# A written-out instruction order replaced in a fused attention and feed-forward kernel on Trainium2, with a new rule for its filler products

## The chip, the cores and the metric

The kernel runs on one core of one Trainium2 chip. The metric is the device time of one execution in microseconds (us); the median of three runs of the kernel before is 267.36 us (266.87 to 269.35). [...]

## The reference, cut to what matters

Eight batches, eight heads, 576 rows of 64 elements. The attention goes by 32 landmarks (the means of 18 rows each), a pseudo-inverse by six Newton steps, and a two-layer network follows on all 4608 rows of 512 elements.

```python
A  = softmax(scale * q @ k_lm.T)          # 576 x 32
Bm = softmax(scale * q_lm @ k_lm.T)       # 32 x 32
C  = softmax(scale * q_lm @ k.T)          # 32 x 576
Z  = Bm.T / (norm1(Bm) * norminf(Bm) + 1e-6)
for _ in range(6):
    Z = 2 * Z - Z @ Bm @ Z
x = A @ Z @ C @ v                         # per head, then heads side by side
h = x @ w_in                              # 512 -> 2048
out = relu(h) ** 2 @ w_out                # 2048 -> 512
```

## The kernel before, in words

The program is a list of named operations. `Plan.op` records each with its engines and what it reads and writes; `Plan.schedule` walks the long string `ORDER`, gives each name a start by a table of costs, and sorts by that start; then each engine's instructions are emitted in that order. A word `R2.7/D` puts the operation on VectorE, `/A` on ScalarE, `/P` on GpSimd; `@2,0` names the banks of the accumulator memory (eight in all). So the string decides three things: the order on every engine, which engine does an operation that has a choice, and which bank is used.

Per batch b the operations are, by name: `ldq`, `ldk`, `ldv`, `lx` (loads, all issued by GpSimd, 16-bit copies of 32-bit inputs), `lm`, `lmc`, `lme`, `lmt` (landmark sums, their copies and transposition), `T` (VectorE transposition of q and k), `B..` (softmax of Bm and its norms), `bd`, `N`, `U` (one Newton step: block-diagonal copy, product, update), `SS` or `SC`, `SA` (scores), `C..` and `A..` (their softmaxes), `CV`, `Zm`, `ZC`, `W`, `We` (the chain C v, Z C v, and its product with w_in, copied to the tile WP). Then the network: `Fb.f` is a group of four products of AT and WP (line 1023), `R` the relu that takes it out of the accumulator (ScalarE line 1037, VectorE line 1039), `Q` the square (line 1046 on VectorE or GpSimd, line 1044 on ScalarE). `Ot.g` is a quarter of the second layer for one tile of 128 rows: four products of 512 columns (line 1063), `Oe` its copy out, `St` its store. Groups `O` of an earlier batch are placed between the groups `F` and the attention of a later one, so that TensorE has work while the other engines do softmaxes.

Constants are made at the start: `c0` and `c1` (memsets of ones, lines 320 and 321), `c2` (GpSimd's affine select that makes the identity, line 322), `c3` (its 16-bit copy, line 325), `c5` (two selects that make a mask, lines 330 and 332). The first landmark product `lm0.1` (line 480) needs that identity, the load `ldq0.1` and the load `ldk0.1`.

Between the kernel's own products stand products of a constant tile of ones (line 1137) that nobody reads, so that TensorE is not idle at the start. `Plan.fillers` chooses them: it takes every gap of the planned TensorE times up to the first group `O0.0`, and fills it with as many as fit.

Of the kernel before, what the change touches and what calls it, by code (L numbers as in the profile page):

```python
# [7 lines left out]
P = 128  # L8
# [45 lines left out]
class Plan:  # L54
# [100 lines left out]

    def fillers(self, until, width, emit):

        busy = sorted((o.start, o.start + o.engs["PE"] + 0.04) for o in self.ops if o.eng == "PE")
        found, at = [], 1.5
        for a, b in busy:  # L160
            if a > until:
                break
            n = int((a - 0.05 - at) / (width if at > 6 else 2 * width))
            if n > 0:
                for j in range(8):
                    if all(h[1] >= a or h[2] <= at - 0.02 for h in self.history if h[0] == j):
                        found.append((at, j, n))
                        break
            at = max(at, b)
        for at, j, n in found:  # L170
            o = Op()
            o.name, o.eng, o.start, o.mode = f"fill{at:.0f}", "PE", at, "full"
# [1003 lines left out]
lmt1.0 bk1/P win20 ldk2.1 B1@4 Asb0.1a ldv1.00 U0.1 Bmx1 Asu0.1b N0.2@0 Arc0.0b U0.2 Bsb1 Aex0.1a
Bex1 CR0@7 CRe0/A Asu0.1a N0.3@6 U0.3 N0.4@7 Bsu1 Arc0.1a CT0.0 U0.4 Brc1 Aex0.0a Asu0.0a Bmb1
Bml1 N0.5@7 U0.5 Arc0.1b Blo1 CV0@0,4 Btr1 Aml0.0b Arc0.0a c14/A CVe0.0/A Bcs1@3 Zd0@6 Zm0
CVe0.1/A ZC0@0 BBT1@2 ZCe0 Aml0.0a Bnm1 T1.01 Bad1 Brn1 Aml0.1b Ap0.0@3 Ab0.0/A SA1.1@6 Aml0.1a
Zi1 Yi1 T1.11 W0.0@0 We0.00 We0.01 N1.0@5 W0.1@2 We0.1 U1.0 T1.10 N1.1@4 U1.1 F0.2@0 R0.2 Amx1.1  # L1180
N1.2@5 U1.2 ldv1.10 Q0.2/P wout0 F0.0@2 R0.0 wout1 Asb1.1 Aex1.1 SC1.0@4,0 Cmx1.1 Ap0.1@2 Ab0.1/A
Cex1.1 N1.3@7 U1.3 Cmx1.0 Cex1.0 SA1.0@6 Amx1.0 N1.4@7 U1.4 Asb1.0 F0.4@2 F0.16@0 R0.4 R0.16
N1.5@7 U1.5 Crc1 W0.3@4 We0.3 Asu1.1 Cmk1 Arc1.1 Aml1.1 F0.18@6 F0.6@0 CR1@2 CRe1 F0.22@4 Q0.16/A
Q0.0/P R0.6 Q0.4/P R0.18/D CT1.0 CT1.1 R0.22 Q0.22/A F0.12@2 R0.12 Aex1.0 W0.2@0 We0.2/D Ap1.1@6
Ab1.1 lm2.0@4 lmc2.00 lmc2.01 lme2.0 CV1@2,0 CVe1.0/A CVe1.1/A F0.20@6 Zd1@2 T2.11 Zm1 F0.26@4
wout2 Q0.6/P R0.20 Q0.20/A F0.10@0 R0.10 ZC1@2 T2.10 ZCe1.0/D lmt2.0 F0.8@6 wout3 Q0.18/P R0.8
lx3.0 Q0.12/P R0.26 Q0.10/A ldv3.11 lx3.1 ldv2.00 ldq3.1 Q0.8/P O1.0@3 F0.14@0 ZCe1.1/D W1.1@6
B2@4 Asu1.0 Arc1.0 Aml1.0 Bmx2 O0.0@2 O0.1 We1.1 Q0.26/A R0.14 Bsb2 Bex2 Bsu2 Brc2 Bml2 Btf2 T2.01
Q0.14 Bcs2 Bct2 Bnm2 Bad2 Brn2 Zi2 W1.2@4 W1.3@6 W1.0@0 We1.2 We1.01 We1.3 We1.00 Btr2/A bt2/D
O1.1 O0.2 Ap1.0@4 F0.28@6 R0.28/D Q0.28/P O1.2 Ab1.0/A F1.0@0 R1.0 F0.24@4 R0.24 T2.00 BBT2@6 Yi2  # L1190
Q0.24 O1.3 Oe1.0 F1.2@0 R1.2/D F0.30@4 St1 R0.30 Q1.0/A F1.6@6 F1.8@0 bd2.0 N2.0@4 U2.0 bd2.1 R1.6
O2.0@5 O0.3 N2.1@4 F1.14@6 Q1.2/A R1.8 U2.1 Q1.8 ldk3.0 bd2.2/D O2.1 N2.2@4 Oe0.0 F1.12@2 F1.4@0
Q0.30/A R1.4 R1.14/D U2.2 bd2.3/D N2.3@4 U2.3 Q1.6 R1.12 O2.2 ldv3.10 bd2.4 ldk3.1 ldv2.11 ldq3.0
lm3.0@4 lme3.0/D lmt3.0 ldv2.10 lx4.0 N2.4@0 U2.4 bd2.5/D Q1.4/A Q1.12/A F1.18@6 R1.18 Q1.18/A
O2.3 F1.10@6 R1.10 Oe2.0 N2.5@4 B3@2 Q1.14 F1.24@0 F1.20@6 Bmx3 Bsb3 U2.5 Bex3 Bsu3 Brc3 Bml3 Btf3
Bcs3 R1.24 Q1.10/A ldv3.00 lx4.1 Zm2.0 Btr3 O3.0@3 O3.1 R1.20 Q1.20/A Q1.24/A SS2.0@0,4,6 T3.10
O5.0@2 O5.1 At2.0 Zm2.3 Amx2.0 Asb2.0 Aex2.0 SS2.1@6 Cmx2.1 Cmx2.0 Cex2.1 At2.1 Cex2.0 Bct3 Bnm3
T3.01 T3.00 Bad3 Crc2.1 Zm2.1 Amx2.1 Cnr2.1 CT2.1 Asb2.1 T3.11 O5.2 O3.2 O3.3 F1.26@6 R1.26 Oe3.0
F1.30@0 F1.22@4 Asu2.0 R1.30/D Crc2.0 F1.16@6 R1.16 Q1.16/A R1.22 O5.3 O4.0@7 O4.1 Aex2.1 Asu2.1
St2 St0 F1.28@4 O4.2 O4.3 Arc2.0 Zm2.2 Arc2.1 Aml2.0 Q1.22/A Oe5.0 R1.28 Q1.30/A Q1.26/A Oe4.0  # L1200
SS3.0@4,0,2 O7.0@6 O7.1 At3.0 Aml2.1 SS3.1@2 Cnr2.0/A CT2.0 At3.1 O6.0@7 O6.1 bt3 BBT3@2 O7.2
Cmx3.1 Ab2.1 Brn3 Yi3 Q1.28/A Cex3.1 CV2@2,0 Cmx3.0 Cex3.0 Amx3.0 Zi3 O7.3 CVe2.0 CVe2.1/A ZC2@0
ZCe2.0/D ZCe2.1 ldk4.0 ldq4.0 bd3.0 ldq5.1 N3.0@1 U3.0 Ab2.0 lm4.0@2 lx5.0 Oe7.0 St4 St5 St3
W2.0@4 We2.0 W2.1@0 We2.1 bd3.1/D N3.1@3 U3.1 bd3.2/D lme4.0/D O6.2 F2.2@4 R2.2 F2.1@2 R2.1 lmt4.0
Crc3.0 Amx3.1 Asb3.1 F2.0@0 R2.0 Q2.0 Q2.1/A O6.3 N3.2@6 U3.2 W2.2@2 W2.3@4 We2.3 We2.2 B4@0
# [24 lines left out]
Q4.2/A Q4.3/A Q4.4/A Cmx5.0 Cex5.0 Cmx5.1 Cex5.1 O17.0@6 O17.1 B6@4 Bmx6 O17.2 Bsb6 Bex6 O16.3  # L1230
Oe16.0 St16 F4.6@2 R4.6 Crc5.0 Cnr5.0 Bsu6 Brc6 N5.5@0 U5.5 Crc5.1 Bml6 F4.5@4 O17.3 F4.8@2 Amx5.1
# [70 lines left out]
```

## Time and profile before

| | us |
|---|---|
| median of three runs | 267.36 |
| lowest and highest | 266.87, 269.35 |
| the profiled execution's own time | 268.07 |
| its span in the trace | 266.3 |
| TensorE busy | 254.8 |
| VectorE busy | 210.7 |
| ScalarE busy | 185.9 |
| GpSimd busy | 75.1 |

In the profile's rows PE is TensorE, PEld its weight loads, DVE is VectorE, ACT is ScalarE, POOL is GpSimd and SP is SyncE, which issues the stores. A busy TensorE is one that has a product in its pipeline, not one at its peak. A row of the view by stretches gives, for each engine, busy time and the number of instructions, then the granted TensorE clock as a share, the share of the sixteen DMA engines, and GB/s. The chain of waits is the work that ended last, followed back from the last instruction.

### The profile page before, as it was taken

Reading aid. Unit: us, or ns where it says so; the run is one execution under the profiler, and the core shown is the slowest. Engines: PE = TensorE matmul, PEld = TensorE weight load, DVE = VectorE, ACT = ScalarE, POOL = GpSimd, SP = SyncE. Lnnn points to the kernel's source line nnn. Section 1 sums busy time; section 2 is a strip of 40 time slices with the busy share of each in tenths; the row PEclk is TensorE's granted clock in tenths of the full one; section 3 lists DMA queues with packets and bytes.
Section 4 is the critical chain, followed back from the end, with each engine's and each line's share of the span. In section 5 each row is a group of like instructions: output and inputs, shape, how many; then the busy total and the mean of one; then the engine's idle time right before and its main releaser. Section 6 shows DMA issues by size and latency. Waiting matters only on the chain.

```text
span 266.3 us, 7555 instructions
## 1 busy us (share of the span) xinstructions
PE 254.8 (96%) x3090; PEld 140.4 (53%) x3090; DVE 210.7 (79%) x539; ACT 185.9 (70%) x339; POOL 75.1 (28%) x121
## 2 busy tenths in 40 slices
PE   7699899999999999999999999999999999999993
PEld 2265566466454566455444556456454555456552
DVE  3399999856899889897998889888899895787311
ACT  1055599978687799899597759899586847667120
POOL 8445389346400362026423220210032102000000
PEclk9799999999999999999999999999999999999999
DMA  5999999997998699919996993213250330017016
GB/s 89 195 196 208 203 201 190 205 182 116 157 234 160 120 165 210 182 41 186 225 224 104 193 178 98 47 15 79 51 114 2 83 81 0 2 34 164 2 47 151
DMA packets 25123, 34.18 MB, mean 128 GB/s; under 512 B 2432, under 2 KB 14464, under 8 KB 25088
## 3 DMA queue, kind: packets, MB, share of 16 engines
q0 software_dynamic: 19168, 24.25, 55.7%
q1 hardware_dynamic: 5840, 9.38, 13.8%
q8 instruction: 24, 0.39, 0.6%
q10 hardware_dynamic: 80, 0.07, 0.1%
q14 instruction: 11, 0.09, 0.1%
HBM read 48.50 MB, written 9.44 MB: 218 GB/s over the span
## 4 chain that ended last, share of the span: by engine, by line
PE 73%; DVE 13%; ACT 6%; issue 3%; DMA 3%; POOL 0%; DVEq 0%; POOLq 0%; ACTq 0%
PE ps L1063 40%; PE ps L1023 20%; ACT RS L1037 3%; DMA X<-in_k_dram 3%; PE ps L859 2%; PE ps L702 2%; DVE TT L442 2%; PE ps L788 2%; ACT G L1044 2%; PE ps L1137 1%; DVE sm L740 1%; DVE WP L388 1%; DVE ST L680 1%; PE ps L666 1%; DVE An L938 1%
## 5 line engine op out<-in xcount | busy, mean ns | idle before, releaser
L1063 PE MATMUL ps<-w_out,G 128*128 128x512 bf16 (+1 forms) x592 | 138.5, 374 | 0.1
L1063 PEld LDWEIGHTS <-G 128*128 128x128 bf16 x592 | 54.1, 98 | 53.3 <-issue 5.4
L1023 PE MATMUL ps<-AT,WP 128*128 128x288 bf16 (+2 forms) x512 | 75.0, 286 | 0.9 <-DVE AT L996 0.3
L1037 ACT ACTIVATE RS<-ps 128x576 bf16<-128x576 f32 (+2 forms) x97 | 60.9, 652 | 19.3 <-PE ps L1023 12.0
L1023 PEld LDWEIGHTS <-WP 128*128 128x128 bf16 x512 | 47.9, 98 | 23.8 <-issue 4.3
L1044 ACT ACTIVATE G<-RS 128x576 bf16<-128x576 bf16 (+2 forms) x78 | 52.3, 687 | 0.7
L603 POOL TENSOR_TENSOR BD<-ST,blkb 128x256 bf16<-128x256 bf16 x21 | 14.9, 710 | 85.6 <-DVE ST L680 44.1
L384 ACT COPY OS<-ps 128x512 f32<-128x512 f32 (+2 forms) x29 | 16.2, 567 | 16.7 <-PE ps L1063 16.5
L442 DVE STREAM_TRANSPOSE TT<-X 128x576 uint32<-128x576 uint32 x32 | 23.8, 758 | 5.1 <-DMA X<-in_k_dram 2.8
L1039 DVE TENSOR_SCALAR RS<-ps 128x576 bf16<-128x576 f32 (+2 forms) x31 | 23.1, 754 | 5.4 <-PE ps L1023 5.1
L384 ACT CAST WP<-ps 128x1024 bf16<-128x1024 f32 (+1 forms) x25 | 22.8, 949 | 3.3 <-PE ps L859 3.2
L743 ACT ACTIVATE C<-ps,sm 128x576 bf16<-128x576 f32 x16 | 14.2, 905 | 12.8 <-DVE sm L740 10.8
L1046 DVE TENSOR_TENSOR G<-RS 128x576 bf16<-128x576 bf16 (+2 forms) x42 | 18.8, 452 | 3.6 <-ACT RS L1037 3.4
L680 DVE SCALAR_TENSOR_TENSOR ST<-ST,ps 128x128 bf16<-128x128 bf16 (+1 forms) x48 | 12.7, 264 | 8.2 <-PE ps L666 8.0
L1137 PE MATMUL ps<-onesb 128*128 128x512 bf16 (+1 forms) x40 | 14.1, 470 | 1.8 <-DVE onesb L320 1.5
L413 POOL DMA_DIRECT2D V<-in_v_dram x24 | 13.0, 543 | 7.5 <-DMA X<-in_q_dram 3.5
L388 DVE COPY OS<-ps 128x512 f32<-128x512 f32 (+1 forms) x9 | 5.8, 640 | 10.8 <-PE ps L1063 9.4
L740 DVE TENSOR_REDUCE sm<-ps 128x1 f32<-128x576 f32 x16 | 11.7, 747 | 1.6 <-PE ps L702 1.6
L976 DVE STREAM_TRANSPOSE SA<-ps 128x320 f32<-128x320 f32 (+1 forms) x24 | 10.1, 459 | 3.5 <-PE ps L697 2.4
L603 POOL TENSOR_TENSOR BD<-Bt,blkb 128x256 bf16<-128x256 bf16 x4 | 3.0, 744 | 30.9 <-DVE sm L597 15.0
L1046 POOL TENSOR_TENSOR G<-RS 128x512 bf16<-128x512 bf16 (+1 forms) x8 | 8.8, 1101 | 9.3 <-DVE RS L1039 5.9
L388 DVE CAST WP<-ps 128x1024 bf16<-128x1024 f32 x9 | 10.8, 1205 | 0.8 <-PE ps L859 0.8
(139 smaller groups left out, 303.9 us busy)
## 6 DMA issues: line engine op xcount, KB each, us to landing
out_dram<-OS SPq DMA_DIRECT2D x70, 128.0 KB, 2.4
X<-in_q_dram POOLq DMA_DIRECT2D x16, 288.0 KB, 9.2
X<-in_k_dram POOLq DMA_DIRECT2D x16, 288.0 KB, 9.3
XS<-in_q_dram POOLq DMA_DIRECT2D x5, 576.0 KB, 11.0
XS<-in_k_dram POOLq DMA_DIRECT2D x5, 576.0 KB, 10.2
V<-in_v_dram POOLq DMA_DIRECT2D x8, 288.0 KB, 10.0
w_in<-in_moe_w_in_dram POOLq DMA_DIRECT2D x8, 256.0 KB, 10.6
w_out<-in_moe_w_out_dram POOLq DMA_DIRECT2D x4, 512.0 KB, 10.2
```

The source lines that it names most:

```text
L384: nc.scalar.copy(o, i)
L388: eng(e).tensor_copy(o, i)
L442: op(f"T{b}.{t}{r}", {"DVE": v_(576)}, lambda e, r=r: nc.vector.transpose(tt[:, t, r].rearrange("p s m e -> p (s m e)").bitcast(U32), x[:, ...
L603: bdiag = lambda e, o, i: eng(e).tensor_tensor(o.rearrange("p r (c m) -> p r c m", c=4), i.unsqueeze(2).to_broadcast([P, 2, 4, M]), blkb[: ...
L680: nc.vector.scalar_tensor_tensor(out=o, in0=i0, scalar=2.0, in1=bank(pN)[:, 0:2 * w].rearrange("p (r w) -> p r w", r=2), op0=ALU.mult, op1 ...
L1023: nc.tensor.matmul(ps[:, ph.at + i, 0:w], lhsT=wp[:, r, 128 * ff:128 * ff + 128], rhs=at[:, r, t0:t0 + w], start=(r == 0), stop=(r == 1))
L1037: nc.scalar.activation(rs, pair(ph, w), AF.Relu)
L1039: nc.vector.tensor_scalar(out=rs, in0=pair(ph, w), scalar1=0.0, scalar2=None, op0=ALU.max)
L1044: nc.scalar.activation(g, rs, AF.Square)
L1046: eng(e).tensor_tensor(g, rs, rs, ALU.mult)
L1063: nc.tensor.matmul(bank(po)[:, 0:c1 - c0], lhsT=G[:, f, lo:lo + P], rhs=w_out[:, f, c0:c1], start=(f == 0), stop=(f == NF - 1))
L1137: nc.tensor.matmul(ps[:, j, 0:w], lhsT=onesb[:, 0:P], rhs=onesb[:, 0:w], start=True, stop=True)
```

## The change

Three things are changed. The string `ORDER` is replaced as a whole: 1421 names that stand in both, in another order, and some on another engine or bank. In it the identity's select `c2` stands behind the second load. The rule of `fillers` is replaced: it gives each TensorE operation a weight (`USE`), looks at windows of 3.41 us of the plan, and adds products to the widest gap of the emptiest window until each window's weighted share is 0.42 or no gap is left.

```diff
+    USE = {"N": 0.06, "M": 0.06, "B": 0.06, "Bce": 0.28, "Bcs": 0.3, "BBT": 0.08, "SC": 0.2, "CR": 0.06, "lm": 0.48,
+           "SA": 0.78, "CV": 0.63, "Zd": 0.6, "ZC": 0.2, "Ap": 0.54, "W": 0.9}
     def fillers(self, until, width, emit):
-        busy = sorted((o.start, o.start + o.engs["PE"] + 0.04) for o in self.ops if o.eng == "PE")
-        found, at = [], 1.5
-        for a, b in busy:
-            if a > until:
-                break
-            n = int((a - 0.05 - at) / (width if at > 6 else 2 * width))
...
+        times = [6.5 + 0.25 * i for i in range(int(4 * (until - 10)))]
+        for _ in range(80):
+            t = min(times, key=share)
+            near = [g for g in gaps if t <= g[0] < t + 3.41 and g[3] - g[0] - g[1] * g[4] > -0.05]
+            if share(t) >= 0.42 or not near:
                 break
+            g = max(near, key=lambda g: g[3] - g[0] - g[1] * g[4])
+            g[1] += 1
...
-c0 ldq0.1 c1 c2 ldk0.1 c3 lm0.1@2 lmc0.10 c12 T0.01 c17 Bce0@5 ldq0.0 ldk0.0 ldq1.0 ldk1.0 c5
+c0 ldq0.1 c13 c17 ldk0.1 ldq0.0 ldk0.0 ldq1.0 c1 c5 Bce0@0 c2 c3 lm0.1@2 c12 c6 c15 ldk1.0 ldk1.1
```

Behind the new rule line numbers are 19 higher, 18 at the end of the file: line 397 before is line 416 after.

On GpSimd, at the start of the program, before:

```order
6 L397 DMA X_62<-in_q_dram 128x1152
7 L322 ISA
8 L322 AFFINE_SELECT identf<-onesf 128x128
9 L397 DMA X_62<-in_k_dram 128x1152
10 L397 DMA X_62<-in_q_dram 128x1152
11 L397 DMA X_62<-in_k_dram 128x1152
12 L397 DMA X_63<-in_q_dram 128x1152
```

and after:

```order
6 L416 DMA X_62<-in_q_dram 128x1152
7 L416 DMA X_62<-in_k_dram 128x1152
8 L416 DMA X_62<-in_q_dram 128x1152
9 L416 DMA X_62<-in_k_dram 128x1152
10 L416 DMA X_63<-in_q_dram 128x1152
11 L349 ISA
12 L349 AFFINE_SELECT msel<-onesf 128x4
13 L351 AFFINE_SELECT msel<-msel 128x4
14 L341 AFFINE_SELECT identf<-onesf 128x128
```

The string names the select behind the second load, but its planned start puts it behind five loads and the mask's two selects.

On TensorE, right behind the first landmark product, before (`Bce` is line 569; four products of ones):

```order
98 L480 MATMUL ps<-X_62,ident 64x128
99 L569 MATMUL ps<-tiny,onesf 128x64
100 L1137 LDWEIGHTS onesb
101 L1137 MATMUL ps<-onesb 128x512
102 L1137 LDWEIGHTS onesb
103 L1137 MATMUL ps<-onesb 128x512
104 L1137 LDWEIGHTS onesb
105 L1137 MATMUL ps<-onesb 128x512
106 L1137 LDWEIGHTS onesb
107 L1137 MATMUL ps<-onesb 128x512
108 L702 LDWEIGHTS LT_75
```

and after, from the third product of ones on:

```order
102 L1156 LDWEIGHTS onesb
103 L1156 MATMUL ps<-onesb 128x512
104 L1156 LDWEIGHTS onesb
105 L1156 MATMUL ps<-onesb 128x512
106 L1156 LDWEIGHTS onesb
107 L1156 MATMUL ps<-onesb 128x512
108 L1156 LDWEIGHTS onesb
109 L1156 MATMUL ps<-onesb 128x512
110 L1156 LDWEIGHTS onesb
111 L1156 MATMUL ps<-onesb 128x256
112 L721 LDWEIGHTS LT_75
```

There are now six products of 512 columns and one of 256 in this place, and `Bce` stands behind the program's very first product of ones. Ahead of the landmark product are eleven of 512 and one of 256, where thirteen stood. In all there are 33 of 512 and 9 of 256, where 33 and 7 stood.

On VectorE, from the first Newton state of batch 2 (`ST_0_97<-ps`) on, before:

```order
131 L627 TENSOR_TENSOR ST_0_97<-ps,sm_118 128x2x32
132 L1046 TENSOR_TENSOR G<-RS_125 128x2x320
133 L1039 TENSOR_SCALAR RS_127<-ps 128x512
134 L680 TENSOR_SCALAR ST_1_98<-ST_0_97,ps 128x128
135 L680 TENSOR_SCALAR ST_0_97<-ST_1_98,ps 128x128
136 L1046 TENSOR_TENSOR G<-RS_127 128x2x256
137 L603 TENSOR_TENSOR BD_101<-ST_0_97,blkb 128x256
138 L1039 TENSOR_SCALAR RS_127<-ps 128x512
139 L680 TENSOR_SCALAR ST_1_98<-ST_0_97,ps 128x128
```

and after:

```order
134 L646 TENSOR_TENSOR ST_0_97<-ps,sm_118 128x2x32
135 L1058 TENSOR_SCALAR RS_127<-ps 128x512
136 L1065 TENSOR_TENSOR G<-RS_126 128x2x256
137 L1058 TENSOR_SCALAR RS_125<-ps 128x640
138 L1065 TENSOR_TENSOR G<-RS_125 128x2x320
139 L699 TENSOR_SCALAR ST_1_98<-ST_0_97,ps 128x128
140 L622 TENSOR_TENSOR BD_102<-ST_1_98,blkb 128x256
141 L699 TENSOR_SCALAR ST_0_97<-ST_1_98,ps 128x128
142 L622 TENSOR_TENSOR BD_101<-ST_0_97,blkb 128x256
```

VectorE takes one relu and one square more ahead of the first Newton update (line 680, then 699), and one block-diagonal copy that GpSimd made before.

More of the change, by code (lines that the diff above doesn't have):

```diff
@@ L1176 @@
[L1176 to L1193, printed above, removed]
@@ L1267 @@
+St34 St35 St31 Oe32.0 St32 O35.5 O35.6 O35.7 Oe35.2 Oe35.3 St35.2 St35.1
 """
```

199 lines of the change are left out of this document (114 added, 85 removed).

## The prediction

> **What bounds the kernel now.** I read the page's head first, then busy time by stretches, then the chain of waits and the timeline of the first 17 us. The head (busy time of TensorE; the chain's shares by engine):
>
> ```profile
> span 266.3 us, 7555 instructions
> PE 254.8 (96%) x3090; PEld 140.4 (53%) x3090; DVE 210.7 (79%) x539; ACT 185.9 (70%) x339; POOL 75.1 (28%) x121
> ...
> PE 73%; DVE 13%; ACT 6%; issue 3%; DMA 3%; POOL 0%; DVEq 0%; POOLq 0%; ACTq 0%
> ```
>
> TensorE is busy nearly throughout and carries 73% of the chain; VectorE carries 13%. An average says nothing about place, so busy time by stretches comes next (the second number is the stretch, then each engine's busy time and count):
>
> ```profile
> 45.00:60.00 15.00, 14.80 (x137) 8.59 (x136) 11.26 (x29) 13.11 (x24) 6.83 (x10) 1.00 1.14 194
> 60.00:70.00 10.00, 10.00 (x132) 5.75 (x131) 6.68 (x24) 8.76 (x16) 6.38 (x12) 1.00 0.85 131
> 70.00:92.00 22.00, 21.96 (x306) 10.45 (x305) 20.35 (x50) 15.81 (x30) 3.08 (x5) 1.00 0.94 175
> 92.00:109.20 17.20, 16.92 (x231) 10.66 (x231) 16.07 (x45) 16.27 (x29) 6.24 (x11) 1.00 1.07 182
> 109.20:132.00 22.80, 22.75 (x242) 12.31 (x241) 18.94 (x51) 18.69 (x33) 8.71 (x14) 1.00 0.79 150
> 144.50:174.00 29.50, 28.89 (x403) 15.55 (x402) 25.72 (x68) 23.79 (x43) 6.36 (x10) 1.00 0.70 128
> ```
>
> From 45 us on TensorE hardly idles. The stretch from 92 to 109 us differs: VectorE and ScalarE are both busy for 16 of 17.2 us, so there they set the pace. To learn how much a better order could win at all, I count TensorE's own work behind 50 us from pieces of the chain (start, duration, what):
>
> ```profile
> 50.85 1.83 PE ps L1063 x8
> ...
> 89.77 0.77 PE ps L458 x24
> ...
> 109.18 0.49 PE ps L1023 x4
> ...
> 112.87 0.77 PE ps L859 x24
> ...
> 131.86 2.59 PE ps L1063 x12
> ...
> 140.06 0.76 PE ps L788 x71
> ...
> 248.00 13.87 PE ps L1063 x80
> ```
>
> Between 50.85 and 248.00 us, 197.2 us, stand by the order 115 groups `F` at 0.49 us, 127 groups `O` at 2.59/3 = 0.863, six `CV` at 0.76, five `lm` at 0.77, 27 `W` at 0.77/3 = 0.26, and small products that I put at 8: 56.4 + 109.6 + 4.6 + 3.9 + 7.0 + 8 = 189.5. Some 7.7 us are lost there in many short stalls. That is the ceiling of what a new order can win behind 50 us. The last stretch, 13.87 us of second-layer products, holds sixteen whole groups and four half ones in both orders, so nothing is won or lost there.
>
> Before 45 us the program is a chain of latencies. Its start in the chain, then the clock in single microseconds (the third number from the right is the granted clock, then the DMA engines' share), then the timeline:
>
> ```profile
> 2.12 0.24 POOL identf L322
> 2.36 6.80 DMA X<-in_k_dram
> ...
> 9.30 0.70 PE ps L480 x36
> ...
> 10.36 1.69 PE ps L1137 x4
> ...
> 13.18 0.76 DVE sm L740
> ```
>
> ```profile
> 2.00:3.00 1.00, 1.00 (x4) 0.38 (x3) 0.50 (x2) 0.09 (x1) 0.91 (x4) 1.00 0.38 32
> 3.00:4.00 1.00, 1.00 (x3) 0.30 (x2) 0.00 (x0) 0.00 (x0) 1.00 (x3) 1.00 0.96 168
> ...
> 11.00:12.00 1.00, 1.00 (x7) 0.16 (x8) 0.90 (x2) 0.00 (x0) 0.80 (x3) 0.50 1.14 214
> 12.00:13.00 1.00, 1.00 (x17) 0.40 (x16) 0.00 (x0) 0.00 (x0) 0.54 (x1) 0.50 1.10 207
> ```
>
> ```profile
> 1.52 5.59 PE L1137 MATMUL ps<-onesb 128*128 128x512 bf16 x13 [1.52 <-DVE onesb L320]
> ...
> 9.30 0.70 PE L480 MATMUL ps<-X,ident 64*64 64x128 bf16 x36 [2.19 <-DMA X<-in_k_dram]
> ...
> 10.20 1.85 PE L1137 MATMUL ps<-onesb 128*128 128x512 bf16 x4
> ...
> 10.99 0.24 DVE L511 STREAM_TRANSPOSE LT<-LM 128x64 uint32<-128x64 uint32 x1
> ...
> 11.98 1.15 PE L702 MATMUL ps<-TT,LT 32*32 32x288 bf16 x16
> ...
> 14.97 1.02 PE L1137 MATMUL ps<-onesb 128*128 128x512 bf16 x4 [0.25 <-ACT C L743]
> ...
> 15.99 0.68 PE L702 MATMUL ps<-TT,LT 32*32 32x288 bf16 x15
> ```
>
> The second load sets the first landmark product, at 9.30. The landmarks are transposed by 11.23 (10.99 + 0.24), but the scores that need them start at 11.98, behind four products of ones that took 1.85 us. The clock was 0.50 there; at full clock four take 1.02, and the scores 0.68 instead of 1.15.
>
> **The change part by part.** *The identity's select.* The select stood between the two loads; without it `ldk0.1` is issued at the end of the first issue, about 0.3 us earlier (2.36 less the chain's 0.24 and some waiting). The bounds are a gain of 0.3 and nothing: the DMA engines have a share of 0.38 between 2 and 3 us, so the load has room to start, but 0.96 right behind, which can eat it. I take 0.3, since the free row is the one that it moves into. What it is moved past: four more loads and the mask's selects. Five issues from 1.31 us on at some 0.55 end near 4.3, the mask and the identity then take 0.8, the copy on VectorE 0.2: the identity is ready near 5.3 us, and the first landmark product at 9.0 covers that by 3.7 us. The three loads behind the selects are issued at most 0.5 us later; they land behind five others and nothing waits for them yet.
>
> *The filler products.* Ahead of the landmark product eleven and a half stand instead of thirteen, with `Bce` among them: 5.59/13 = 0.43 us each, the pause behind them stays at about 2 us, and so should the low clock. Behind it stand six and a half instead of `Bce` and four. At the low clock 1.85/4 = 0.46 us each, 6.5 of them take 3.0 us: from 9.0 + 0.7 = 9.7 to 12.7, where the scores began at 11.98. Less the first product's latency (1.85 is 1.69 in the chain, so 0.42 each, 12.45) the scores start 0.5 us later, with the 0.3 already used. At full clock (1.02/4 = 0.26) they end at 11.4, and the scores take 0.68: that is 0.6 earlier and 0.5 shorter, a gain of 1.1. Bounds: +0.5 and -1.1. I take +0.5, the row of this execution, since the pause in front of it stays. From there VectorE is the engine that all wait for, up to about 31 us, and its operations up to the first Newton update of batch 1 are the same but for one exchange with ScalarE of 0.28 us; so the shift reaches the end whole. The other fillers sum to about the same, and stand in waits for VectorE.
>
> [...]
>
> *The order on VectorE and ScalarE.* This is the large part. The groups of a relu, a square, a copy of the output and the block-diagonal copy, on each engine (busy, mean ns):
>
> ```profile
> L1037 ACT ACTIVATE RS<-ps 128x576 bf16<-128x576 f32 (+2 forms) x97 | 60.9, 652 | 19.3 <-PE ps L1023 12.0
> ...
> L1044 ACT ACTIVATE G<-RS 128x576 bf16<-128x576 bf16 (+2 forms) x78 | 52.3, 687 | 0.7
> L603 POOL TENSOR_TENSOR BD<-ST,blkb 128x256 bf16<-128x256 bf16 x21 | 14.9, 710 | 85.6 <-DVE ST L680 44.1
> L384 ACT COPY OS<-ps 128x512 f32<-128x512 f32 (+2 forms) x29 | 16.2, 567 | 16.7 <-PE ps L1063 16.5
> ...
> L1039 DVE TENSOR_SCALAR RS<-ps 128x576 bf16<-128x576 f32 (+2 forms) x31 | 23.1, 754 | 5.4 <-PE ps L1023 5.1
> ...
> L1046 DVE TENSOR_TENSOR G<-RS 128x576 bf16<-128x576 bf16 (+2 forms) x42 | 18.8, 452 | 3.6 <-ACT RS L1037 3.4
> ...
> L388 DVE COPY OS<-ps 128x512 f32<-128x512 f32 (+1 forms) x9 | 5.8, 640 | 10.8 <-PE ps L1063 9.4 <-ACT OS L384 1.4
> ...
> L603 DVE TENSOR_TENSOR BD<-ST,blkb 128x256 bf16<-128x256 bf16 x15 | 4.2, 283 | 0.2
> ```
>
> Over the whole program eight squares of 576 columns go from ScalarE to VectorE, and seven block-diagonal copies from GpSimd: 8 x 0.687 = 5.5 us less on ScalarE, 8 x 0.452 + 7 x 0.283 = 5.6 more on VectorE; against that four copies of WP and three of tiles of the output go the other way. The engines' sums end near where they were, and the change lies in the places. Up to the first reduction of batch 3, near 67 us before, VectorE has by the order four relus, one square and two block-diagonal copies more: 4 x 0.754 + 0.452 + 2 x 0.283 = 4.0 us. Its idle time between 45 and 92 us is 47 - 38.3 = 8.7 us, so this cover can hold it; it would then be 90% busy, and what is late next is the Newton chain of batch 2, whose result is wanted only near 90 us. Between 92 and 109 us, where the two engines set the pace, VectorE is by the order two relus and three block-diagonal copies lighter and three squares and one copy of the output heavier: -2 x 0.754 - 3 x 0.283 + 3 x 0.452 + 0.640 = 0.4 us less. ScalarE has those two relus more and the squares and the copy less: 2 x 0.652 - 3 x 0.687 - 0.567 = 1.3 us less. The mean of the two, 0.8, is my gain for that stretch. For the rest I take nothing: everywhere else TensorE idles under 3% of a stretch, and the new places are as full as the old. The bounds are a gain of the whole 7.7 us of stalls, and a loss of the 4.0 us that VectorE gets, if its idle time is all waiting for TensorE's results and can't be used.
>
> The sum on the profiled execution: 268.07 + 0.5 - 0.8 = 267.8. That execution stands 0.7 us above the median of the runs, so the forecast is 267.36 - 0.3 = 267.1 us.
>
> **The rivals.** *The clock stays full at the start.* [...] Then -1.1 replaces +0.5: 267.1 - 1.6 = 265.5 us.
>
> *ScalarE's relief dissolves the stalls.* If the stalls behind 50 us come from squares that ScalarE does late, the lighter ScalarE saves about half of the 7.7 us, 4 instead of 0.8: 267.1 - 3.2 = 263.9 us. For it speaks that ScalarE is the slower at a square (0.687 against 0.452); against it that outside the stretch at 92 us it idles for an eighth to a quarter of its time.
>
> *VectorE is overfull.* The other side: the 4.0 us that VectorE takes over before 70 us find no room, because its idle time there is waiting for `F` and `N` products, and the work queues up in front of batch 2's softmaxes. From 70 to 92 us VectorE is busy for 20.35 of 22 us already, so what is left over at 70 us can't be caught up before TensorE needs C v of batch 2. It decides from the point where VectorE absorbs less than 3 of the 4.0 us; with nothing absorbed, the time is 267.1 + 4.0 = 271.1 us.
>
> **How the numbers follow.** I give the forecast as worked out 0.55, the full clock 0.16, the relieved ScalarE 0.13, and the overfull VectorE 0.16. About 1% of the time, 2.7 us, is what a measurement of this kernel can tell from no change: faster is below 264.7, slower above 270.0. The first two cases lie inside, 0.71; the third is faster, 0.13; the fourth slower, 0.16. The range reaches down to the third case with some measuring error, 263.6, and up to 270.4, short of the fourth, so that about 0.16 is left out.
>
> **What would show it right or wrong.** In the profile after: the issue of the second load near 2.05 us and the first landmark product near 9.0 show the first term. The scores of line 721 starting near 12.5, behind the products of line 1156, at a clock of 0.50, show the second; a clock of 1.00 there shows the first rival. VectorE busy for about 42 of the 47 us from 45 to 92, with TensorE still idle for less than 0.5 us, shows that the idle time held the work; TensorE waiting for VectorE there shows the last rival. The network of batch 2 taking some 0.8 us less than 17.2 shows the third term. The forecast is wrong if TensorE loses or gains more than 3 us between 50 and 248 us, since I priced most of the new places at nothing from their occupancy alone.

## The result and the profile after

The new kernel takes 265.36 us (median of 4 runs, 264.03 to 266.00) where the kernel before takes 268.36 (4 runs on the same chip, 266.87 to 270.69): a ratio of 0.990, 95% interval 0.986 to 0.994. Run once more beside the last experiments it took 263.74 us (5 runs, 263.38 to 264.76) beside 268.32 (23 runs): 0.984, interval 0.981 to 0.987. So it is faster, by 1.0 to 1.6%; the forecast was 0.3 us. A ratio here leaves out single disturbed runs of either kernel, so it isn't always the quotient of two medians.

The profiled run took 264.03 us. Its head, to be laid beside that of before (busy time, then the chain's shares by engine):

```profile
span 262.3 us, 7508 instructions
PE 248.2 (95%) x3053; PEld 140.7 (54%) x3092; DVE 208.9 (80%) x551; ACT 184.6 (70%) x334; POOL 70.3 (27%) x114
...
PE 64%; DVE 12%; ACT 8%; DMA 8%; issue 4%; POOL 2%; SPq 2%; POOLq 0%; DVEq 0%; ACTq 0%
```

The span is 4.0 us shorter. TensorE's busy time can't be compared so simply: the trace after has 3053 records of products where there are 3092 weight loads, so 39 are missing, 35 of them second-layer products, and part of the 6.6 us less is that. DMA has gone from 3 to 8% of the chain. Why shows in the chain of waits of the first 20 us of the new kernel (start, duration, what):

```profile
1.30 2.84 POOL X L416 x5
4.14 0.06 POOLq L349 x2
...
4.70 0.24 POOL identf L341
4.94 1.05 POOL X L416 x2
5.99 10.64 DMA X<-in_q_dram
16.63 0.14 issue
16.77 2.13 PE ps L492 x18
```

Before, this chain waited for the second load (2.36 to 9.16). Now it runs through eight issues on GpSimd to the last of the eight loads of batches 0 and 1, which lands at 16.63, and into the landmark product of batch 1. The second load is off the chain: in the timeline of the new kernel,

```profile
1.30 0.71 POOL L416 DMA_DIRECT2D X<-in_q_dram  x1 [0.79 <-POOLq L1304]
...
2.02 0.54 POOL L416 DMA_DIRECT2D X<-in_k_dram  x1
...
2.24 3.88 PE L1156 MATMUL ps<-onesb 128*128 128x512 bf16 x11
...
7.01 0.70 PE L499 MATMUL ps<-X,ident 64*64 64x128 bf16 x36 [0.89 <-DMA X<-in_k_dram]
...
7.86 1.35 PE L1156 MATMUL ps<-onesb 128*128 128x512 bf16 x6 [0.16 <-issue]
...
9.14 0.69 PE L721 MATMUL ps<-TT,LT 32*32 32x288 bf16 x16
```

It is issued at 2.02 instead of 2.36, but it lands at 6.87 instead of 9.16. The first landmark product starts 2.29 us earlier (7.01), TensorE's pause ahead of it is 0.89 instead of 2.19 us, and the scores start at 9.14 instead of 11.98 and take 0.69 instead of 1.15. The clock belongs to this. Busy time by stretches, before, then after (the third number from the right is the granted clock):

```profile
7.00:9.00 2.00, 0.11 (x1) 0.00 (x0) 0.00 (x0) 0.00 (x0) 0.22 (x1) 1.00 1.06 173
9.20:10.20 1.00, 0.90 (x39) 0.84 (x40) 0.89 (x2) 0.16 (x1) 0.62 (x1) 1.00 1.09 198
10.30:13.60 3.30, 3.30 (x24) 1.00 (x22) 1.90 (x5) 0.01 (x1) 1.50 (x4) 0.50 1.11 208
13.70:15.00 1.30, 1.05 (x19) 0.93 (x18) 1.30 (x3) 1.03 (x4) 0.50 (x1) 1.00 1.10 209
```

```profile
7.00:9.00 2.00, 1.83 (x42) 1.14 (x43) 1.71 (x6) 0.27 (x1) 0.68 (x2) 1.00 1.08 200
9.20:10.20 1.00, 0.95 (x18) 0.35 (x17) 0.96 (x3) 0.00 (x0) 0.63 (x1) 1.00 1.09 203
10.30:13.60 3.30, 2.48 (x53) 1.63 (x53) 2.74 (x8) 1.14 (x4) 1.19 (x3) 1.00 1.10 208
```

Before, the trace's record of the clock has one window of 3.41 us at 0.50 (10.25 to 13.66), right behind one of 3.41 us at 1.00 (6.84 to 10.25) in which the pause lies (7.11 to 9.30); TensorE got through 24 products in it, where the new kernel, with other products, does 53 between the same times. Up to the last product the new kernel's profile has no such window.

Operation by operation, TensorE is ahead of the kernel before by 2.83 us at the first scores, 2.29 at batch 1's landmarks, 2.49 at the first group `F`, 3.32 at the first scores of batch 2 and 3.83 at the last product (257.75 us instead of 261.58). So some 60% of the gain were made in the first 20 us.

### The profile page after: what moved, and what is told of

The parts are those of the page before. It is cut to its first block, busy times and chain, and to the rows that moved or that the text cites. A ratio compares the mean times of both kernels' runs of the same rounds, so it can differ in the third digit from the quotient of the medians.

```text
span 262.3 us, 7508 instructions
## 1 busy us (share of the span) xinstructions
PE 248.2 (95%) x3053; PEld 140.7 (54%) x3092; DVE 208.9 (80%) x551; ACT 184.6 (70%) x334; POOL 70.3 (27%) x114
## 3 DMA queue, kind: packets, MB, share of 16 engines
q1 hardware_dynamic: 5840, 9.38, 13.8%
## 4 chain that ended last, share of the span: by engine, by line
PE 64%; DVE 12%; ACT 8%; DMA 8%; issue 4%; POOL 2%; SPq 2%; POOLq 0%; DVEq 0%; ACTq 0%
PE ps L1082 35%; PE ps L1042 17%; DMA X<-in_q_dram 4%; DMA out_dram<-OS 4%; PE ps L878 3%; ACT RS L1056 2%; ACT G L1063 2%; PE ps L807 2%; SPq L1095 2%; PE ps L721 2%; POOL X L416 1%; DVE RS L1058 1%; DVE An L1012 1%; ACT C L762 1%; PE ps L477 1%
## 5 line engine op out<-in xcount | busy, mean ns | idle before, releaser
L1082 PE MATMUL ps<-w_out,G 128*128 128x512 bf16 (+1 forms) x557 | 133.9, 373 | 2.9 <-issue 1.4
L1056 ACT ACTIVATE RS<-ps 128x576 bf16<-128x576 f32 (+2 forms) x96 | 59.4, 652 | 11.2 <-PE ps L1042 7.3
L1063 ACT ACTIVATE G<-RS 128x576 bf16<-128x576 bf16 (+2 forms) x69 | 46.6, 690 | 4.0 <-DVE RS L1058 3.3
L403 ACT CAST WP<-ps 128x1024 bf16<-128x1024 f32 (+1 forms) x28 | 25.9, 971 | 9.1 <-PE ps L878 9.0
L403 ACT COPY OS<-ps 128x512 f32<-128x512 f32 (+2 forms) x32 | 18.0, 569 | 18.6 <-PE ps L1082 17.6
L622 POOL TENSOR_TENSOR BD<-ST,blkb 128x256 bf16<-128x256 bf16 x14 | 9.8, 702 | 68.7 <-DVE ST L699 57.3
L1065 DVE TENSOR_TENSOR G<-RS 128x576 bf16<-128x576 bf16 (+2 forms) x51 | 22.3, 451 | 7.2 <-ACT RS L1056 6.8
L407 DVE COPY OS<-ps 128x512 f32<-128x512 f32 (+1 forms) x6 | 3.8, 625 | 14.1 <-DMA out_dram<-OS 8.7
L1156 PE MATMUL ps<-onesb 128*128 128x512 bf16 (+1 forms) x38 | 11.9, 407 | 2.0 <-DVE onesb L339 1.5
L878 PE MATMUL ps<-w_in,ZC 64*32 64x512 bf16 x256 | 10.6, 383 | 0.0
```

Of the source, the lines that this page charges most:

```text
L403: nc.scalar.copy(o, i)
L622: bdiag = lambda e, o, i: eng(e).tensor_tensor(o.rearrange("p r (c m) -> p r c m", c=4), i.unsqueeze(2).to_broadcast([P, 2, 4, M]), blkb[: ...
L878: nc.tensor.matmul(ps[quad(pos_a(c, r)), pW.at + r, :], lhsT=zcs[r][half, pos_c(c, r), :], rhs=w_in[half, c, 512 * ch:512 * ch + 512], sta ...
L1056: nc.scalar.activation(rs, pair(ph, w), AF.Relu)
L1063: nc.scalar.activation(g, rs, AF.Square)
L1065: eng(e).tensor_tensor(g, rs, rs, ALU.mult)
```

## Experiments

Each kernel is compared with runs of the kernel before on the same chip; 1 to 4, 5 to 8 and 9 to 12 share one each. In the edits only the beginning of a line of the string is shown, and operations and limits that the text describes are left out. "The select" is the identity's (`c2`). In the rows the first landmark product is the one with `ident 64*64`, whatever its line; batch 1's is the one with `128x256`.

**1. The select right behind the second load.**

```diff
-c0 ldq0.1 c1 c2 ldk0.1 c3 lm0.1@2
+c0 ldq0.1 c1 ldk0.1 c2 c3 lm0.1@2
```

> The kernel before with the identity's select moved behind the second load, nothing else. Theory A (the select between the two loads holds up the second load's data, not only its issue): the second load lands near 7.0 us instead of 9.16, the first landmark product follows the thirteen products of ones at about 7.1, and the whole is 2.0 to 2.8 us faster than before. Theory B (only the 0.3 us of issue are saved, the rest of the new kernel's early start comes from its other order): landing near 8.9, time 0.3 us less.

Measured: 266.35 us (10 runs) beside 267.56, ratio 0.997 (0.994 to 1.000). Its timeline:

```profile
2.02 0.55 POOL L397 DMA_DIRECT2D X<-in_k_dram  x1
2.65 0.32 POOL L322 TENSOR_SCALAR_AFFINE_SELECT identf<-onesf 128x128 f32<-128x128 f32 x1
...
7.22 0.70 PE L480 MATMUL ps<-X,ident 64*64 64x128 bf16 x36 [0.90 <-DMA X<-in_k_dram]
...
8.12 1.03 PE L1137 MATMUL ps<-onesb 128*128 128x512 bf16 x4
9.21 0.69 PE L702 MATMUL ps<-TT,LT 32*32 32x288 bf16 x16
```

The landing (7.08) and the clock are theory A's; one move of one instruction gives the new kernel's start. But only 1.2 us of it arrive in the medians, 0.8 by the ratio, whose interval just reaches no change; in the two profiled runs it is 1.87, the same within 0.03 at every operation from 39 us to the end. Batch 1's landmark product takes the difference:

```profile
17.55 2.12 PE L473 MATMUL ps<-X,ident 128*128 128x256 bf16 x18 [0.69 <-DMA X<-in_k_dram]
```

It waits for the eighth load, 1.50 us ahead of the kernel before where the scores were 2.77 ahead.

**2. The select put back into the new kernel.**

```diff
-c0 ldq0.1 c13 c17 ldk0.1 ldq0.0 ldk0.0 ldq1.0 c1 c5 Bce0@0 c2 c3 lm0.1@2
+c0 ldq0.1 c1 c2 ldk0.1 c13 c17 ldq0.0 ldk0.0 ldq1.0 c5 Bce0@0 c3 lm0.1@2
```

> The new kernel with the identity's select (and the memset that it reads) put back between the first two loads; body order, banks, engines and filler products stay the new ones. Theory A: the second load lands near 9.2 again, the first landmark product goes back to about 9.3 and the gain is lost: within 0.8 us of the kernel before. Theory B: 0.3 us slower than the new kernel, so still 2.5 us faster than before.

Measured: 267.58 us (10 runs) beside 267.56, ratio 1.000 (0.996 to 1.003): the whole gain is gone, more than experiment 1 won. Its timeline:

```profile
8.86 1.18 PE L499 MATMUL ps<-X,ident 64*64 64x128 bf16 x36 [3.06 <-DMA X<-in_k_dram]
...
9.97 2.95 PE L1156 MATMUL ps<-onesb 128*128 128x512 bf16 x7
...
12.85 1.15 PE L721 MATMUL ps<-TT,LT 32*32 32x288 bf16 x16
```

The second load lands at 8.72, the clock is 0.50 for 6.83 us (7.93 to 14.75), the longer row of products of ones takes 2.95 us, and the scores start 0.87 later than before the change. In this profile the late load comes with a low clock of 6.83 us, 3.41 in the kernel before, and with the longer row, and the new order wins some of it back: TensorE is 0.94 us behind the kernel before at the first group `F` and 0.27 at the last product.

**3. The old filler rule in the new kernel** (the method `fillers` of before, nothing else).

> The new kernel with the old rule for the filler products. The first 31 products of ones stand in the same places by either rule, so theory A and theory B both expect the time of the new kernel within 0.5 us, 2.5 to 3 us faster than before; if the rule by the share of use in a window is worth something, the time goes up by more than 0.5 us.

Measured: 265.00 us (10 runs), ratio 0.992 (0.988 to 0.995); the new kernel's own two results are 0.990 and 0.984, from other sets of runs. The interval overlaps that of the first and not that of the second, so the rule by itself is worth nothing that shows clearly, and up to 0.8% is not excluded. The longer row behind the landmarks comes from the string, whose plan leaves a longer gap there.

**4. VectorE quiet while the second load is issued.**

```diff
-c0 ldq0.1 c1 c2 ldk0.1 c3 lm0.1@2 lmc0.10 c12 T0.01 c17
+c0 ldq0.1 c1 c2 ldk0.1 T0.01 c3 c12 lm0.1@2 lmc0.10 c17
```

(and at most eight half products in the two gaps behind, so that their numbers stay).

> The kernel before with the select between the two loads, but VectorE's copy of the identity and its memset of cpick moved from the second load's issue (2.46 to 2.96 us) to behind the first transposition, so VectorE does nothing while GpSimd issues that load (one product of ones fewer ahead of the first load's own landmark product). Theory A1 (the select itself is at fault): the second load still lands at 9.2, time as before. Theory A2 (VectorE's work during the issue holds up the load's descriptors): it lands near 7.2, time 2 us or more below before.

Measured: 267.06 us (10 runs), ratio 0.998 (0.995 to 1.001), landing 9.22. Timeline:

```profile
2.36 0.59 POOL L399 DMA_DIRECT2D X<-in_k_dram  x1
...
6.28 0.18 DVE L327 CAST ident<-identf 128x128 bf16<-128x128 f32 x1
...
9.35 0.70 PE L482 MATMUL ps<-X,ident 64*64 64x128 bf16 x36 [2.15 <-DMA X<-in_k_dram]
...
10.25 1.72 PE L1139 MATMUL ps<-onesb 128*128 128x512 bf16 x4
```

In this profile VectorE is not at fault. In the kernel before, the copy of the identity falls just into that issue (2.46 us); here it runs 3.8 us later, at 6.28, and the second load lands at 9.22 instead of 9.16.

**5 and 6. A gap without the select.** A memset on GpSimd in the select's place, and an issue that only waits for a memset of its target on VectorE (the string as in 5); in both the select stands behind the second load.

```diff
+    op("g0", {"POOL": 0.57}, lambda e: nc.gpsimd.memset(identf[:], 0.0), W=["identf"])
...
-c0 ldq0.1 c1 c2 ldk0.1 c3 lm0.1@2
+c0 ldq0.1 c1 g0 ldk0.1 c2 c3 lm0.1@2
```

```diff
+    op("g0", {"DVE": 0.6}, lambda e: nc.vector.memset(X[0][:, 1, 1, :, :], 0.0), W=[("X", 0, 1, 1)])
```

> As the run with the select behind the second load, but GpSimd does a memset of 128x128 32-bit elements between the first two loads, where the select stood. [...] Theory A3 (it is the select, or the configuration instruction ahead of it): landing 0.1 to 0.3 later than the 7.08 of that run, time as there, 1.2 us less than before.

> GpSimd does nothing between the first two loads, but the second load's issue waits for a memset on VectorE of the tile that it fills, to about 2.3 us; the select stands behind it. Theory A2 (the gap): landing 8.5 to 9.3 as with the select, time as before. Theory A3 (the instruction): landing near 7.3, 0.3 later than without the wait, time about 1 us less than before.

Measured (beside 268.64 us): with the memset 266.48 us (10 runs), ratio 1.000 (0.996 to 1.004), landing 6.82; with the wait 268.04 (10 runs), ratio 1.003 (0.999 to 1.007), landing 7.84. The memset's timeline, then the wait's:

```profile
2.03 0.22 POOL L322 MEMSET identf<- 128x128 f32 x1
2.17 0.55 POOL L398 DMA_DIRECT2D X<-in_k_dram  x1
...
6.96 0.70 PE L481 MATMUL ps<-X,ident 64*64 64x128 bf16 x36 [0.85 <-DMA X<-in_k_dram]
```

```profile
2.53 0.54 POOL L398 DMA_DIRECT2D X<-in_k_dram  x1 [0.50 <-DVE X L325]
...
7.98 0.70 PE L481 MATMUL ps<-X,ident 64*64 64x128 bf16 x36 [1.81 <-DMA X<-in_k_dram]
8.88 1.03 PE L1138 MATMUL ps<-onesb 128*128 128x512 bf16 x4
```

With the wait the second load is issued 0.17 later than behind the select and lands 1.3 earlier. A gap of 0.50 us alone costs about 1.1 (2.57 behind the first load's landing instead of 1.36 to 1.52); what is more, 0.9 to 1.8 us, goes with the select. The memset leaves a gap of only 0.15, so it speaks against an instruction of GpSimd as such, not against the gap. The times settle nothing: with the memset the medians are 2.2 us apart, the ratio says 1.000. In the profiled runs the memset's kernel is 2.41 us ahead of the kernel before to the end; the wait's is 1.94 ahead at batch 0's first `W` product, and a window of low clock at 28.82 takes 1.07 of it.

**7. Five more products of ones ahead of the first landmark product**, meant to fill the pause while the load stays late (`if at < 2: n += 10` in `fillers`).

> The kernel before, select between the loads, with five more products of ones ahead of the first landmark product, so that TensorE has no pause of 2.19 us there; the load's landing stays at 9.2. Theory C (the low clock came from the pause alone): the clock stays 1.00 from 9 to 14 us, the four products behind the landmarks take 1.02 instead of 1.85 and the scores 0.69 instead of 1.15; the scores start near 11.3 instead of 11.98; time 0.7 us, up to 1.1, below before. [...]

Measured: 268.14 us (10 runs) beside 268.64, ratio 1.003 (0.998 to 1.008). The pause is not filled. The eighteen products end at 7.78, and TensorE still waits for 1.74 us:

```profile
1.53 6.25 PE L1139 MATMUL ps<-onesb 128*128 128x512 bf16 x18 [1.53 <-DVE onesb L322]
...
9.52 0.70 PE L482 MATMUL ps<-X,ident 64*64 64x128 bf16 x36 [1.74 <-DMA X<-in_k_dram]
...
10.42 1.03 PE L1139 MATMUL ps<-onesb 128*128 128x512 bf16 x4
```

In this profiled run (266.94) the rest is as theory C has it: no window at 0.50, the four products take 1.03, the scores 0.69 (11.51 on), and everything behind 33 us is 0.96 earlier, although the load landed at 9.38. Taken with the others, low windows began in pauses of 3.01 us and more ahead of that product (2 and 9) or some 1 us behind pauses of 2.15 and 2.19 us (4 and the kernel before), and none did with 1.81 us (6), 1.74 (7) or less; that is one profile each, and a start without any pause was not tried with a late load. Over the runs nothing is left of the gain: only 3 of 10 ran at a clock of 0.999 or more.

**8. The new kernel's order on GpSimd in the kernel before.**

```diff
-c0 ldq0.1 c1 c2 ldk0.1 c3 lm0.1@2 lmc0.10 c12 T0.01 c17 Bce0@5 ldq0.0 ldk0.0 ldq1.0 ldk1.0 c5
-ldq1.1 ldk1.1
+c0 ldq0.1 ldk0.1 ldq0.0 ldk0.0 ldq1.0 c1 c5 c2 c3 lm0.1@2 lmc0.10 c12 T0.01 c17 Bce0@5 ldk1.0 ldk1.1
+ldq1.1
```

> The kernel before with the new kernel's order on GpSimd up to the eighth load (five loads, the mask's selects, the identity's select, three loads); the rest of the string, engines, banks and the filler rule are the old ones. With the select right behind the second load the time was 1.2 us below before (1.9 in the profiled pair). Theory D (0.8 us of that run's early start were given back to the loads of batch 1, which landed 0.8 later than in the new kernel): 2.0 us below before in the medians, 2.5 to 2.7 in the profiled run, the rest up to the new kernel being body order. Theory E (all that is left over comes from the body's order): as that run, 1.2 and 1.9.

Measured: 266.11 us (10 runs) beside 268.64, ratio 0.993 (0.989 to 0.996), 1.9 us. That is theory D's time, but the interval, 1.0 to 2.9 us, does not exclude theory E's 1.2. The trace speaks for D: batch 1's landmark product starts at 16.84 instead of experiment 1's 17.55, and the lead at batch 0's first `W` product is 2.62 us, 1.88 in experiment 1. From 33 us to the end it is only 1.55; in between lies a window at half clock that the kernel before does not have there. Stretches of this kernel, then one of before:

```profile
26.00:28.00 2.00, 1.71 (x25) 1.02 (x23) 1.97 (x8) 0.59 (x1) 0.54 (x1) 1.00 1.19 208
28.20:31.40 3.20, 3.20 (x40) 1.33 (x40) 2.50 (x7) 2.52 (x4) 1.02 (x2) 0.50 1.17 209
31.60:33.60 2.00, 2.00 (x53) 1.23 (x51) 1.38 (x3) 1.46 (x3) 2.00 (x3) 1.00 1.18 205
```

```profile
28.20:31.40 3.20, 3.06 (x59) 1.82 (x58) 3.17 (x11) 1.47 (x4) 0.66 (x2) 1.00 1.18 207
```

So one such window costs 1.07 us here.

**9 and 10. What of the select it is.** In the order on GpSimd an `ISA` stands ahead of the first select, of `identf` before and of `msel` after, where the two selects behind it have none; the expectations call it the configuration instruction. In 9 a tiny memset and a 128x1 select stand ahead of the first load, so that the identity's is no longer the first select; in 10 the mask's 128x4 select stands between the first two loads and the identity's behind the second.

```diff
-c0 ldq0.1 c1 c2 ldk0.1 c3 lm0.1@2
+c0 g0 ldq0.1 c1 c2 ldk0.1 c3 lm0.1@2
```

```diff
-c0 ldq0.1 c1 c2 ldk0.1 c3 lm0.1@2
+c0 ldq0.1 c1 g0 ldk0.1 c2 c3 lm0.1@2
```

> The kernel before with a tiny memset and a tiny select (128x1) on GpSimd ahead of the first load, so that the configuration instruction, which comes ahead of a program's first select, is over before any load; the identity's select stays between the first two loads. All loads are issued some 0.4 us later, so the second load's landing less the first's is compared (3.9 us in the kernel before, 1.4 to 1.5 with nothing or a memset between). Theory A3a (the configuration instruction holds up the descriptors): 1.5 to 2.0. Theory A3b (the select itself does): 3.4 to 4.2.

> The mask's first select (128x4 elements, 0.24 us) between the first two loads, with the configuration instruction ahead of it, and the identity's select (128x128, 0.31 us) between the second and the third. If the configuration instruction or any select holds up the load behind it, the second load lands 3.4 to 4.2 us behind the first, as in the kernel before. If the size of the select counts, below 2.5 us, and the third load, behind the identity's select, is then the late one.

Measured (beside 268.32 us): 9 took 268.11 us (10 runs), ratio 0.995 (0.992 to 0.999), second landing 4.34 behind the first; 10 took 267.15 (10 runs), ratio 0.997 (0.994 to 1.000), 2.72 behind. The timeline of 9:

```profile
2.17 0.30 POOL L327 TENSOR_SCALAR_AFFINE_SELECT identf<-onesf 128x128 f32<-128x128 f32 x1
2.42 0.58 POOL L402 DMA_DIRECT2D X<-in_k_dram  x1
...
9.90 1.17 PE L485 MATMUL ps<-X,ident 64*64 64x128 bf16 x36 [3.01 <-DMA X<-in_k_dram]
```

The identity's select is the second one here (2.17, behind the 128x1 at 0.98), and the load behind it is still 4.34 us behind the first, 3.90 in the kernel before; so in this profile the instruction ahead of the first select is not what makes it late. The small select settles nothing: 2.72 lies in neither expected range; it is near the 2.57 of the wait, though its gap is 0.23 us and not 0.50; and the third load, behind the identity's select, landed only 1.43 behind the second.

**11. The selects behind all eight loads, in the new kernel** (and as many products of ones behind the landmarks as there).

```diff
-c0 ldq0.1 c13 c17 ldk0.1 ldq0.0 ldk0.0 ldq1.0 c1 c5 Bce0@0 c2 c3 lm0.1@2 c12 c6 c15 ldk1.0 ldk1.1
-ldq1.1 T0.01 T0.11
+c0 ldq0.1 c13 c17 ldk0.1 ldq0.0 ldk0.0 ldq1.0 ldk1.0 ldk1.1
+ldq1.1 c1 c2 c5 Bce0@0 c3 lm0.1@2 c12 c6 c15 T0.01 T0.11
```

> The new kernel with its three selects behind all eight loads of batches 0 and 1 (they stand behind five). The identity is then ready near 7 us, just when the first landmark product starts. If the selects behind the fifth load still hold up the last of the eight (it landed at 16.63 in the new kernel, 1.5 us behind the spacing of 1.4 us per load), it lands near 15.5 and the time is 0.5 to 1.0 us below the new kernel. If loads that have a backlog ahead of them don't feel a select, landing 16.2 to 16.7 and the time of the new kernel, or 0.1 to 0.2 more for the later identity.

Measured: 264.80 us (6 runs), ratio 0.988 (0.984 to 0.992), eighth landing 16.53 (16.63 in the new kernel). So the selects behind the fifth load are not what makes the eighth late, and nothing is won (264.80 us, where the new kernel took 263.74 on this chip). Here no select stands ahead of any of the eight loads, and still the eighth lands 2.55 us behind the seventh; in experiment 3 the seventh lands 2.95 behind the sixth. A load of the eight can come late without a select next to it, and moving the select brings the second landing forward by more than the eighth: 2.08 and 0.19 us in experiment 1, 2.29 and 0.98 in the new kernel.

**12. The new kernel once more.**

> The new kernel unchanged, for a narrower interval and to count its windows of low clock: 0.988 to 0.993 of before. If the clock's windows make the spread of the runs, runs of granted clock 1.00 lie near 264.0 and each window of 3.41 us at 0.50 adds about 1.1 us.

Measured: 263.74 us (5 runs), ratio 0.984 (0.981 to 0.987), clocks 0.993 to 0.998. It is better than the expected 0.988 to 0.993, and no version here beats it. No run has a clock of 1.000, so the expectation about such runs is not tested. In the profiled run (0.997) the one low window starts at 260.32 us, behind the last product, and costs nothing, so a mean clock just below 1 need not mean a loss.

The start of all of them, from the trace (us; "low" is where the clock is 0.50 in the first 40 us, start and length; the last columns are the starts of three products):

| kernel | between the first two issues | 2nd issue | 1st, 2nd landing | behind by | low | landmarks 0 | scores | landmarks 1 |
|---|---|---|---|---|---|---|---|---|
| before | select | 2.36 | 5.26, 9.16 | 3.90 | 10.25, 3.41 | 9.30 | 11.98 | 19.05 |
| 2 | select | 2.35 | 5.24, 8.72 | 3.48 | 7.93, 6.83 | 8.86 | 12.85 | 20.06 |
| 4 | select, VectorE quiet | 2.36 | 5.55, 9.22 | 3.67 | 10.44, 3.41 | 9.35 | 11.90 | 18.98 |
| 7 | select, pause of 1.74 | 2.37 | 5.27, 9.38 | 4.11 | none | 9.52 | 11.51 | 18.52 |
| 9 | select, configured before | 2.42 | 5.42, 9.76 | 4.34 | 9.58 and 30.06, 3.41 each | 9.90 | 13.19 | 19.80 |
| 10 | small select | 2.25 | 5.22, 7.94 | 2.72 | 27.98, 6.83 | 8.08 | 10.07 | 17.65 |
| 6 | wait | 2.53 | 5.27, 7.84 | 2.57 | 28.82, 3.41 | 7.98 | 9.97 | 17.65 |
| 5 | memset | 2.17 | 5.36, 6.82 | 1.46 | none | 6.96 | 8.95 | 16.99 |
| 1 | nothing | 2.02 | 5.56, 7.08 | 1.52 | none | 7.22 | 9.21 | 17.55 |
| 8 | nothing | 2.03 | 5.52, 6.88 | 1.36 | 28.12, 3.41 | 7.02 | 9.02 | 16.84 |
| 3 | nothing | 2.01 | 5.55, 6.91 | 1.36 | 26.84, 3.41 | 7.05 | 9.18 | 16.59 |
| 11 | nothing | 2.02 | 5.59, 6.96 | 1.37 | 25.93, 3.41 | 7.10 | 9.55 | 16.66 |
| 12 | nothing | 2.02 | 5.55, 6.91 | 1.36 | none | 7.05 | 9.19 | 16.29 |
| after | nothing | 2.02 | 5.51, 6.87 | 1.36 | none | 7.01 | 9.14 | 16.77 |

**The clock over all runs.** Each run lists its mean granted clock. Of 85 runs of the kernel before beside these experiments, 5 had 1.000 and took 265.26 to 266.27 us (median 265.75); 32 between 0.992 and 0.998 took 267.57 in the median, 24 between 0.986 and 0.992 took 268.44, 22 between 0.980 and 0.986 took 269.08, and two below that 270.25 and 270.50. A line through all 85 gives 1.9 us for 0.01 of clock; one window of 3.41 us at 0.50 is 1.71 / 266 = 0.0064 of the mean, so 1.2 us. At a clock of 1.000 experiment 1 took 265.75 in the median (6 of its 10 runs), 8 took 264.96 (3 of 10), and 3, which is the new kernel but for the filler rule, 264.12 and 264.14 (2 of 10). On the chip of experiments 1 to 4 four runs of the kernel before at 1.000 took 265.94 in the median, so there and with the clock whole the select's move alone is worth 0.2 us, nothing that shows, and the whole change without its rule 1.8. On the chip of 5 to 8 there is one such run, 265.26, 0.3 above experiment 8. These are too few to split the rest between the other loads' earlier issue and the new body. By the line, most of the select's 1.2 us in experiment 1 go with windows of low clock that its runs have less often: its mean clock was 0.9952, that of the kernel before beside it 0.9916, which is 0.7 us. Whether the second load was late in those five runs of full clock too is not known; only profiled runs tell a landing.

## Where the prediction was right and where it was wrong, step by step

**The identity's select: failed.** The issue went to 2.02, the 0.3 us earlier that was forecast, and the identity was ready at 5.20, as covered as it was said to be. The step that failed is "I take 0.3": it let the landing move with the issue, and bounded the gain at 0.3. The landing moved by 2.29. Experiments 1 and 2 show that it follows the select's place. By 4, 5, 6 and 9, one profile each, neither VectorE nor the configuration instruction nor a gap alone makes up the whole delay of the load behind it. In the kernel before, four of the sixteen completion signals of that load came between 8.47 and 9.16, the other twelve by 7.39; why they come late stays open. The row that could have warned was in the chain shown: 2.36 + 6.80 is a landing 3.90 us behind the first load's (5.26), where the loads behind it land 1.4 apart.

"The three loads behind the selects ... nothing waits for them yet" failed as well, the other way: batch 1's landmarks wait for the last of them, and take back 0.5 of the 2.8 us in the new kernel, 1.3 in experiment 1.

**The filler products: right for a pause that was not there any more.** The +0.5 rested on "since the pause in front of it stays". With the late load that is what happens: in experiment 2 the scores start 0.87 later, at a clock of 0.50. In the new kernel the pause was 0.89 us and the clock whole, so the term became the rival's: from the landmarks to the scores' end it takes 9.14 + 0.69 - 7.01 = 2.82 us instead of 11.98 + 1.15 - 9.30 = 3.83, a gain of 1.0 where 1.1 was given. That rival, "the clock stays full at the start", had 0.16. It does not take the longer row behind the landmarks: experiment 1 has the old row and a clock of 1.00 in its whole profiled run. As far as single profiles tell, it goes with the shorter pause ahead of them: low windows came with pauses of 2.15 us and more, none there with 1.81 and less.

**The order on VectorE and ScalarE: the size about right, the place wrong.** VectorE was to be busy for some 42 of 47 us in the stretch from 45 to 92 of before, and to hold its 4.0 us more. The two kernels in that stretch, before, then after with the times it has there:

```profile
45.00:92.00 47.00, 46.76 (x573) 24.79 (x571) 38.29 (x103) 37.69 (x68) 16.30 (x25) 1.00 0.98 172
```

```profile
42.50:89.00 46.50, 45.60 (x563) 24.77 (x570) 42.12 (x109) 34.34 (x62) 15.10 (x23) 1.00 0.98 174
...
88.80:106.00 17.20, 16.84 (x232) 11.06 (x233) 14.28 (x39) 15.27 (x26) 6.91 (x12) 1.00 1.08 193
```

42.12 us, and TensorE still idles for only 0.9. The sign named for it was less than 0.5; of the 0.9, 0.73 end at a second-layer product, and the trace misses some of these. So the cover held, and "VectorE is overfull" fell. But the 0.8 us in the stretch of batch 2's network were not there. VectorE and ScalarE are lighter in it, 14.28 and 15.27 us instead of 16.07 and 16.27, yet TensorE does 232 products in 17.2 us where it did 231; from batch 2's first `W` product to batch 3's `CV` it takes 12.84 us, 12.78 before. Those engines did not set the pace. What the body did win, about 1.2 us against experiment 8 in the profiled pair once its low window is taken out (3.83 - 1.53 - 1.07), came in steps between 33 and 150 us. Which of the moves made them was not tried. "ScalarE's relief", 4 us, did not come; as a cause it stays open.

**The sum.** 268.07 + 0.5 - 0.8 was wrong by its start, which came 2.3 to 2.8 us earlier where the sum had it 0.5 later. That the measured 265.36 us lies in the range of 263.6 to 270.4, and near the first rival's 265.5, is luck: the bounds were taken for other reasons, and the rival had the whole clock with a landing only 0.3 us earlier, not 2.29.

## What to carry to other kernels

When a load that the start waits for lands much further behind the load ahead of it than its neighbours are apart (here 3.90 us, and 1.4), look at what its issuing engine does just ahead of it, and price the landing, not the issue. A wait of TensorE at the start may cost twice, as the 2.19 us of the kernel before did: itself, and 3.41 us at a clock of 0.50 behind it. Follow an early start to the next wait, here for the eighth load (1.3 of 2.8 us given back in experiment 1), before it is counted as won; and compare runs at equal granted clock before a difference of 1% is explained.

## What the runs showed of the hardware

- An identity's select of 0.31 us on GpSimd between the first two loads of the queue made the second land 3.5 to 4.3 us behind the first in five kernels, where it was 1.4 to 1.5 with nothing or a memset between, and 2.6 to 2.7 with a wait or a small select. Between the second load and the third it was 2.3, 2.6, 1.4 and 1.4 us with the select, 1.4 to 2.1 without; the load issued right behind selects that follow five or eight loads was not late. Loads came up to 2.95 us behind the one ahead without a select next to them, too. Each is one profile per kernel, and by what the select delays the load's packets stays open.
- In the first 40 us of these profiles the granted clock falls to 0.50 for 3.41 or 6.83 us at a time, or not at all, at places that differ from profile to profile: the low stretch begins in or some 1 us behind the wait for the second load (7.93 to 10.44 us) or among the small products later on (25.93 to 30.06 us). In the kernel before the runs go from 265.26 us at a clock of 1.000 to 270.95 at 0.981, most of their spread.
- From 39 us to the end of the profiled runs the lead over the kernel before stays within 0.03 us in experiment 1 and within 0.06 in 4, 5, 7 and 8; in 6 it drops once, by 0.4 us near 75 us.
